# Queries and keys loaded with their tokens in columns, and split from SBUF, in a fused attention and two-block kernel

## The chip, the core and the metric

The kernel runs on one core of a Trainium2 chip, as one program. The metric is the device time of an execution in microseconds. Three timed runs of the kernel before gave 903.86, 904.44 and 904.83 us, so the median is 904.44.

Engine names in the profile: PE is TensorE (PEld its weight loads), DVE is VectorE, ACT is ScalarE, POOL is GpSimd, SP is the engine whose queue issues every DMA of this kernel.

## The reference

Four batches of eight heads, 576 tokens, 64 columns each; the inputs are float32 except the weights, which are float64. Attention has a causal mask and a decay made from a running sum of log f. Its output, 2304 tokens of 512 columns, goes through two feed-forward blocks.

```python
scores = q @ k.T / sqrt(64)
cum = cumsum(log(clip(f, 1e-4, 1)), -1)
scores = where(causal, -1e9, scores + cum[..., :, None] - cum[..., None, :])
attn = exp(scores - max(scores)); attn = attn / (sum(attn) + 1e-9)
x = (attn @ v).transpose(0, 2, 1, 3).reshape(2304, 512)
h = x @ w_in                                   # 512 -> 1024
solu = h * softmax(h); x = layernorm(solu) * g_ln @ w_out
h = maximum(x @ w2_in, 0); out = h * h @ w2_out  # 512 -> 2048 -> 512
```

Products have to be nearly exact in float32. The kernel gets that by splitting each float32 operand in two: hi, its leading bits, and lo, the rest. Three products, hi by lo, lo by hi and hi by hi, stand for one.

## The kernel before

**Tiles.** A query tile is 128 tokens of one batch, or the 64 that are left over at a seam of two batches: 20 tiles, 16 of 128 tokens and 4 of 64. For each tile the kernel goes through the eight heads. A head has scores (L478), the row's least value (L498), the exponentials with their sum (L512), the division by the sum on GpSimd (L539), transposes of the probabilities (L555) with a copy out of PSUM, and, for two heads at a time, the product with the values (L578). When 128 tokens of x are complete, the first block's work for them follows between the heads of later tiles: w_in (L762 to L764), softmax and norm, transposes (L839), w_out (L703 to L705). The second block (L1034 to L1066) runs after attention; its weights are converted at the seam of the two phases, in the places that keys and others leave.

**Queries and keys.** For scores, TensorE contracts over the 64 columns of a head, so queries and keys must lie with those columns in partitions. `load` (L348) brings a tile's keys, queries and values with tokens in partitions, into KN, QN (two buffers each) and VN. `transposed` (L363) turns four blocks of 128 columns, each holding a pair of heads, on TensorE into one PSUM slot of a ring of three. `prep_k` (L390) and `prep_q` (L426) then make from PSUM what the scores need:

- hi of the even heads and of the odd heads: K1[j] and Q1[i][j], in the pair's own half of the partitions, by a copy on ScalarE or VectorE (the query's one with the scale). The other half of K1 holds two rows of cum, which `auxrows` loads (L411).
- lo of each: K2[j] in the same half, Q2[i][j] in the opposite half, by a subtraction on VectorE (L419, L442).
- a duplicate of hi beside lo: in K2 in the opposite half, in Q2 in the same half, by `dup` (L380) on GpSimd or by a DMA from SBUF to SBUF.

One matmul then contracts hi with hi and the cum rows, and a second one the two cross products.

**The order.** Each instruction is a step of a plan (`Plan`, L28): it names its engine or engines, a duration, a priority, what it reads and what it writes. `lay` puts the steps in time by those durations and by fixed delays between engines, least priority value first among the steps that can start, and each engine and the DMA queue get their instructions in that order. The durations, delays and priorities are the program's own assumptions, and no engine leaves its order at run time: an instruction that waits holds up all behind it on its engine. Where a step can run on several engines, `lay` picks. Keys of the next tile are made from head PK (0) of the current tile on, queries from head PQ (6) on; loads go two tiles ahead.

Of the kernel before, what the change touches and what calls it, by code (L numbers as in the profile page):

```python
# [27 lines left out]
class Plan:  # L28
    """Puts the instructions in the order in which each engine is to take them.

    A step runs on one engine (or one of several), holds it for a time, and names what it reads and
    writes; from these come its dependencies, as if the steps ran in the order they were added. The
    steps are then laid out in time, the least `prio` first among those that can start, and emitted in
    the order of their starts. A step may take a PSUM slot of a ring, free again after its last user.
    """
# [21 lines left out]
    def add(self, eng, fn, prio, reads=(), writes=(), take=None, uses=(), late=0):  # L57
        """eng: {engine: ns}; take: the key of a slot that this step is the first to use; uses: keys of slots;
        late: what its consumers wait beyond the usual, if less then only on other engines."""
# [1204 lines left out]
```

## Time and profile before

| | |
|---|---|
| timed runs, us | 903.86, 904.44, 904.83 |
| profiled execution, span from first to last instruction, us | 902.2 |
| busy TensorE, VectorE, ScalarE, GpSimd, us | 856.1, 504.7, 478.0, 323.0 |
| mean granted TensorE clock | 0.994 |
| DMA queue q1: packets, MB | 97488, 64.88 |
| chain that ended last | PE 78%, DVE 11%, ACT 4%, POOL 3%, issue 3%, DMA 1% |

The profile gives the profiled execution's span and no other time for it; the median of the timed runs lies 2.2 us above it. A busy time counts the stretch from an instruction's start to its end, and TensorE's matmuls overlap, so a busy TensorE need not be one at its peak. In a row of the view by stretch, each engine has its busy us and in brackets the number of instructions. In a row of the timeline, equal instructions that follow each other are merged: start, length up to the last one's end, and the count. A wait row names the instruction that waited and the one that let it go.

### The profile page before, as it was taken

To read this page: it belongs to the slowest core of one execution; us is meant where nothing else is said; L and a number is where in the kernel's file an instruction comes from. 1 tells how busy PE (TensorE), PEld (TensorE's weight loads), DVE (VectorE), ACT (ScalarE), POOL (GpSimd) and SP (SyncE) were. 2 spreads that over 40 slices of the span, in tenths; PEclk is the share of its full clock that TensorE was granted. 3 is DMA by queue.
4 is the path that set the end of the run, shared out by engine and by line. 5 is a ranking of instruction groups with operands and counts; after the bars stand their busy time and mean duration, and the time that the engine had idled before them with its cause. 6 is when DMAs were issued, how large, how long until landed. Compare 5 with 4: busy or idle time off the path is not lost.

```text
span 902.2 us, 15952 instructions
## 1 busy us (share of the span) xinstructions
PE 856.1 (95%) x5440; PEld 734.4 (81%) x5440; DVE 504.7 (56%) x1463; ACT 478.0 (53%) x1242; POOL 323.0 (36%) x502
## 2 busy tenths in 40 slices
PE   4889999999999999999989787999999999999998
PEld 3567787888888888888879676899989999899997
DVE  8998777665776667765599889322222222222221
ACT  6788766667666666665667666223322322322322
POOL 7988743333333444432588778200000000000000
PEclk9999999999999999999999999999999999999999
DMA  8634331122311224010546643005102002000000
GB/s 220 171 99 114 95 84 41 43 65 56 76 42 43 59 62 97 26 48 25 164 144 191 202 139 117 1 1 167 43 1 71 36 1 71 36 1 0 36 1 36
DMA packets 97569, 65.90 MB, mean 73 GB/s; under 512 B 63408, under 2 KB 87472, under 8 KB 97488
## 3 DMA queue, kind: packets, MB, share of 16 engines
q1 hardware_dynamic: 97488, 64.88, 24.7%
q8 instruction: 43, 0.70, 0.3%
q14 instruction: 38, 0.31, 0.1%
HBM read 48.98 MB, written 14.30 MB: 70 GB/s over the span
## 4 chain that ended last, share of the span: by engine, by line
PE 78%; DVE 11%; ACT 4%; POOL 3%; issue 3%; DMA 1%; SPq 0%; POOLq 0%; ACTq 0%; DVEq 0%
PE pp L1034 6%; PE pp L1035 6%; PE pp L1036 6%; PE xo L578 6%; PE z L478 6%; PE pp L555 6%; PE pp L703 3%; PE hp L762 3%; PE hp L764 3%; PE hp L763 3%; PE pp L704 3%; PE pp L705 3%; PE z L1064 2%; PE z L1066 2%; PE hp L1064 2%
## 5 line engine op out<-in xcount | busy, mean ns | idle before, releaser
L1045 DVE CAST q<-q 128x384 fp32r<-128x384 f32 x96 | 40.5, 422 | 252.6 <-PE pp L1066 92.2
L1042 ACT ACTIVATE q<-pp 128x384 f32<-128x384 f32 x96 | 47.0, 490 | 232.4 <-PE pp L1036 230.5
L539 POOL TENSOR_SCALAR adj<-adj,st 128x128 f32<-128x128 f32 (+9 forms) x160 | 92.1, 578 | 176.1 <-DVE st L535 85.4
L512 ACT ACTIVATE adj<-z,st 64x288 f32<-64x288 f32 (+9 forms) x192 | 95.7, 501 | 34.3 <-DVE st L498 20.1
L478 PE MATMUL z<-k,q 128*128 128x256 f32 (+8 forms) x384 | 95.5, 342 | 6.6 <-ACT adj L512 6.4
L278 ACT COPY pt<-pp 128x256 f32<-128x256 f32 (+5 forms) x170 | 69.0, 423 | 48.2 <-PE pp L555 45.6
L703 PE MATMUL pp<-ln,woh 128*128 128x256 f32 x288 | 84.4, 293 | 0.4 <-POOL woh L282 0.4
L555 PE MATMUL pp<-ident,adj 128*128 128x128 f32 (+1 forms) x480 | 77.3, 274 | 6.2 <-POOL adj L539 3.2
L498 DVE CUSTOM_DVE_ANT_0 z<-z,maskb 128x128 f32<-128x128 f32 (+8 forms) x144 | 65.9, 460 | 28.0 <-PE z L478 26.4
L704 PE MATMUL pp<-ln,wol 128*128 128x256 f32 x288 | 81.1, 282 | 0.1
L705 PE MATMUL pp<-ln,woh 128*128 128x256 f32 x288 | 81.2, 282 | 0.0
L555 PEld LDWEIGHTS pp<-ident,adj 128*128 128x128 f32 (+1 forms) x480 | 53.1, 141 | 26.2 <-POOL adj L539 9.9
L578 PE MATMUL xo<-pt,vn 128*64 128x128 f32 (+3 forms) x960 | 73.6, 276 | 0.1
L578 PEld LDWEIGHTS xo<-pt,vn 128*64 128x64 f32 (+1 forms) x960 | 49.0, 136 | 26.1 <-issue 19.0
L478 PEld LDWEIGHTS z<-k,q 128*128 128x128 f32 (+1 forms) x384 | 56.8, 183 | 16.4 <-ACT adj L512 10.7
L762 PE MATMUL hp<-wih,xl 128*128 128x512 f32 x144 | 61.8, 429 | 0.5 <-ACT hp L801 0.5
L764 PE MATMUL hp<-wih,xh 128*128 128x512 f32 x144 | 57.3, 398 | 0.0
L763 PE MATMUL hp<-wil,xh 128*128 128x512 f32 x144 | 57.2, 397 | 0.0
L703 PEld LDWEIGHTS pp<-ln,woh 128*128 128x128 f32 x288 | 54.3, 188 | 2.8 <-issue 1.0
L704 PEld LDWEIGHTS pp<-ln,wol 128*128 128x128 f32 x288 | 54.3, 189 | 0.8 <-DVE wol L637 0.3
L705 PEld LDWEIGHTS pp<-ln,woh 128*128 128x128 f32 x288 | 54.2, 188 | 0.0
L1044 ACT ACTIVATE q<-q 128x384 f32<-128x384 f32 x96 | 50.4, 525 | 2.5
(481 smaller groups left out, 2263.7 us busy)
## 6 DMA issues: line engine op xcount, KB each, us to landing
x2d<-xc SPq DMA_DIRECT2D x72, 128.0 KB
pt<-in_moe_w_in_dram SPq DMA_DIRECT2D x22, 256.0 KB
pt<-in_moe_w_out_dram SPq DMA_DIRECT2D x22, 256.0 KB
ln<-x2d SPq DMA_DIRECT2D x24, 192.0 KB
out_dram<-pt SPq DMA_DIRECT2D x18, 256.0 KB
kn<-in_k_dram SPq DMA_DIRECT2D x16, 256.0 KB
qn<-in_q_dram SPq DMA_DIRECT2D x16, 256.0 KB
vn<-in_v_dram SPq DMA_DIRECT2D x16, 256.0 KB
```

The costliest lines, as they stand in the source:

```text
L278: nc.scalar.copy(dst(), src())
L478: nc.tensor.matmul(dst, lhsT=ql[:, p, 0:m], rhs=rhs, start=(g == 0), stop=(g == 1))
L512: nc.scalar.activation(out=adj[0:m, c[1] : c[2]], in_=Z[c[0]][0:m, 0 : c[2] - c[1]], func=AF.Exp, bias=st[0:m, low : low + 1], scale=-1.0, ...
L539: nc.gpsimd.tensor_scalar(out=adj[0:m, 0:ext], in0=adj[0:m, 0:ext], scalar1=st[0:m, 5:6], scalar2=1.0, op0=ALU.mult, op1=ALU.mult,)
L555: nc.tensor.transpose(at(sk)[:, (c - g) * m : (c - g + 1) * m], adj[0:m, zc : zc + P], ident[0:m, 0:m])
L578: nc.tensor.matmul(XO[own[j], p, off : off + m], lhsT=VN[vslot[b, c]][0:r, (2 * p + j) * D : (2 * p + j + 1) * D], rhs=pts[j][0:r, c * m : ...
L703: nc.tensor.matmul(px, lhsT=woh[:, fc, w], rhs=lo, start=(fc == 0), stop=False)
L704: nc.tensor.matmul(px, lhsT=wol[:, fc, w], rhs=hi, start=False, stop=False)
L705: nc.tensor.matmul(px, lhsT=woh[:, fc, w], rhs=hi, start=False, stop=(fc == KF - 1))
L762: nc.tensor.matmul(HP[:, c], lhsT=XL[i][:, cc, :], rhs=wih[:, cc, w], start=(cc == 0), stop=False)
L763: nc.tensor.matmul(HP[:, c], lhsT=XH[i][:, cc, :], rhs=wil[:, cc, w], start=False, stop=False)
L764: nc.tensor.matmul(HP[:, c], lhsT=XH[i][:, cc, :], rhs=wih[:, cc, w], start=False, stop=(cc == KC - 1))
```

## The change

The program's inputs q and k are handed over with tokens in the last dimension, as [batch, head, 64, 576]; that rearrangement of the inputs is no part of the device's time, and values are as before. `load` brings a tile's keys and queries in two DMAs each, one for the even heads into the lower 64 partitions and one for the odd heads into the upper 64, each row a run of 128 (or 64) tokens. `transposed` and `dup` are gone. `prep_k` and `prep_q` read KN and QN in SBUF instead of PSUM: copies may now go to GpSimd as well, lo is a subtraction of two SBUF operands, the duplicate of a query's hi is a second scaled copy from QN, and every duplicate of a key's hi is a DMA. The head at which queries of the next tile start goes from 6 to 4. Comments were taken out too; most lines of the program move by some 14.

```diff
-    KN = [new(f"kn{i}", [DM]) for i in range(2)]
-    QN = [new(f"qn{i}", [DM]) for i in range(2)]
+    KN = [new(f"kn{i}", [NP, P]) for i in range(2)]
+    QN = [new(f"qn{i}", [NP, P]) for i in range(2)]
...
         def dma(dst, src):
             def fn():
-                nc.sync.dma_start(
-                    dst[0:m].rearrange("p (h d) -> p h d", d=D), src[b, :, q0 : q0 + m, :].rearrange("h s d -> s h d")
-                )
+                for j in range(2):
+                    nc.sync.dma_start(
+                        dst[own[j], :, 0:m], src[b, :, :, q0 : q0 + m].rearrange("(p j) d s -> j d p s", j=2)[j]
+                    )
             return fn
...
-    def transposed(src, m, prio, reads):
...
-    def dup(m, dst, src, prio, reads, writes, by_dma):
...
     def prep_k(n, prio):
...
-        sk, tp = transposed(KN[n % 2], m, prio, [("kn", n % 2)])
+        raw = KN[n % 2]
         for j in range(2):
             rows = slice(0, P) if fresh else own[j]
             copy(
-                NP * m, lambda j=j, rows=rows: K1[j][rows, :, cs], lambda rows=rows: tp()[rows], prio + 1, [sk],
-                kcells("kh", j, kc, kc + m) + (kcells("ka", j, kc, kc + m) if fresh else []), [sk],
+                NP * m, lambda j=j, rows=rows: K1[j][rows, :, cs], lambda rows=rows: raw[rows, :, 0:m], prio + 1,
+                [("kn", n % 2)], kcells("kh", j, kc, kc + m) + (kcells("ka", j, kc, kc + m) if fresh else []),
+                psum=False,
             )
...
-                    out=K2[j][own[j], :, cs], in0=tp()[own[j]], in1=K1[j][own[j], :, cs].bitcast(F32), op=ALU.subtract
+                    out=K2[j][own[j], :, cs], in0=raw[own[j], :, 0:m], in1=K1[j][own[j], :, cs].bitcast(F32),
+                    op=ALU.subtract,
                 )
+            def dup(j=j):
+                nc.sync.dma_start(K2[j][other[j], :, cs].bitcast(F32), K1[j][own[j], :, cs].bitcast(F32))
...
+            pl.add(dict(dma=3.6 * m), dup, prio + 2, hk, kcells("kd", j, kc, kc + m))
...
     def prep_q(n, prio):
...
-        sk, tp = transposed(QN[i], m, prio, [("qn", i)])
         for j in range(2):
             copy(
-                NP * m, lambda j=j: q1[j][own[j], :, 0:m], lambda j=j: tp()[own[j]], prio + 1, [sk], [("qh", i, j)],
-                [sk], SC,
+                NP * m, lambda j=j: q1[j][own[j], :, 0:m], lambda j=j: raw[own[j], :, 0:m], prio + 1, [("qn", i)],
+                [("qh", i, j)], (), SC, False,
+            )
+            copy(
+                NP * m, lambda j=j: q2[j][own[j], :, 0:m], lambda j=j: raw[own[j], :, 0:m], prio + 2, [("qn", i)],
+                [("qd", i, j)], (), SC, False,
             )
...
-                    out=q2[j][other[j], :, 0:m], in0=tp()[own[j]], scalar=SC,
+                    out=q2[j][other[j], :, 0:m], in0=raw[own[j], :, 0:m], scalar=SC,
                     in1=q1[j][own[j], :, 0:m].bitcast(F32), op0=ALU.mult, op1=ALU.subtract,
...
-PK, PQ = 0, 6
+PK, PQ = 0, 4
...
+        if name in ("q", "k"):
+            a = a.transpose(0, 1, 3, 2)
```

The plan makes a new order from these steps. These places show it. Names end in the program's buffer numbers: in the keys' and queries' buffers k_8 and k_9 are K1 of even and odd heads, k_10 and k_11 their K2, q_12 to q_15 are Q1, q_16 to q_19 Q2, kn and qn the loaded tiles.

TensorE in the middle of attention, before: first-block matmuls (L703 to L705), a transposed query tile, and the scores of one head.

```order
L704 MATMUL pp_124<-ln_56_709,wol_74 128x256
L705 MATMUL pp_124<-ln_56_709,woh_73 128x256
L371 MATMUL pp_125<-ident_67,qn_22_89 128x128 x4
L478 MATMUL z_120<-k_8_75,q_14_81 128x288
L478 MATMUL z_120<-k_10_77,q_18_85 128x288
L703 MATMUL pp_124<-ln_56_710,woh_73 128x256
L704 MATMUL pp_124<-ln_56_709,wol_74 128x256
```

The same scores in the changed program, where L689 to L691 are the first-block matmuls and L464 the scores:

```order
L690 MATMUL pp_125<-ln_56_729,wol_74 128x256
L691 MATMUL pp_125<-ln_56_729,woh_73 128x256
L464 MATMUL z_119<-k_8_75,q_14_81 128x288
L464 MATMUL z_119<-k_10_77,q_18_85 128x288
L689 MATMUL pp_125<-ln_56_730,woh_73 128x256
L690 MATMUL pp_125<-ln_56_729,wol_74 128x256
```

The group of four transposes is gone, and the matmuls stand next to each other; the PSUM slot that it took is free for others.

The DMA queue at the start, before (L1105 stores the two parts of cum, L411 loads them into K1, L355 loads queries and keys, L605 words of w_in):

```order
L605 DMA ln_52_170<-in_moe_w_in_dram 128x1024
L355 DMA kn_21_88<-in_k_dram 128x8x64
L1105 DMA cumd<-pt_53_172 32x576
L1105 DMA cumd<-pt_53_177 32x576
L355 DMA qn_23_90<-in_q_dram 128x8x64
L411 DMA k_8_75<-cumd 2x4x128
L411 DMA k_9_76<-cumd 2x4x128
```

And now (L409 is a duplicate of keys, L1091 a store of cum, L357 the loads, L395 the cum rows of K1, L363 values):

```order
L591 DMA ln_52_165<-in_moe_w_in_dram 128x1024
L409 DMA k_10_77<-k_8_75 64x4x128
L1091 DMA cumd<-pt_52_163 32x576
L409 DMA k_11_78<-k_9_76 64x4x128
L357 DMA kn_21_88<-in_k_dram 64x4x128 x2
L1091 DMA cumd<-pt_53_170 32x576
L357 DMA qn_23_90<-in_q_dram 64x4x128 x2
L395 DMA k_8_75<-cumd 2x4x128
L395 DMA k_9_76<-cumd 2x4x128
```

The first tile's duplicates stand ahead of the two stores of cum, and each load of keys or queries is two DMAs.

VectorE at the start, before (L1128 is the running sum, L1134 the lo part of cum, L419 and L442 the subtractions for lo):

```order
L1125 MEMSET adj_30_97 32x576
L1128 SCALAR_TENSOR_TENSOR adj_32_99<-adj_30_97,adj_31_98 32x576
L419 TENSOR_TENSOR k_10_77<-pp_123,k_8_75 64x4x128
L1134 TENSOR_TENSOR pt_53_177<-adj_32_99,pt_53_172 32x576
L419 TENSOR_TENSOR k_11_78<-pp_123,k_9_76 64x4x128
L442 SCALAR_TENSOR_TENSOR q_16_83<-pp_124,q_12_79 64x512
L442 SCALAR_TENSOR_TENSOR q_17_84<-pp_124,q_13_80 64x512
```

And now (L1114, L1120, L403, L432 are the same; L285 is a copy of a key tile's hi):

```order
L1111 MEMSET adj_30_97 32x576
L285 CAST k_9_76<-kn_20_87 128x4x128
L1114 SCALAR_TENSOR_TENSOR adj_32_99<-adj_30_97,adj_31_98 32x576
L403 TENSOR_TENSOR k_10_77<-kn_20_87,k_8_75 64x4x128
L403 TENSOR_TENSOR k_11_78<-kn_20_87,k_9_76 64x4x128
L1120 TENSOR_TENSOR pt_53_170<-adj_32_99,pt_52_163 32x576
L432 SCALAR_TENSOR_TENSOR q_16_83<-qn_22_89,q_12_79 64x512
L432 SCALAR_TENSOR_TENSOR q_17_84<-qn_22_89,q_13_80 64x512
```

A copy of keys moved ahead of the running sum, and both subtractions of the first key tile ahead of the lo part of cum.

The queue in the middle of attention, before (L737 stores x2, L386 is a duplicate of queries):

```order
L737 DMA x2d<-xc_1220 128x256 x2
L355 DMA qn_22_89<-in_q_dram 128x8x64
L355 DMA kn_21_88<-in_k_dram 128x8x64
L737 DMA x2d<-xc_1220 128x256 x4
L355 DMA qn_23_90<-in_q_dram 128x8x64
L386 DMA q_19_86<-q_15_82 64x512
L737 DMA x2d<-xc_1220 128x256 x2
```

And now, at a like place (L723 stores x2, L363 loads values, L409 is a duplicate of keys):

```order
L723 DMA x2d<-xc_1115 128x256 x2
L363 DMA vn_27_94<-in_v_dram 128x8x64
L409 DMA k_10_77<-k_8_75 64x4x128
L409 DMA k_11_78<-k_9_76 64x4x128
L723 DMA x2d<-xc_1115 128x256
L357 DMA kn_20_87<-in_k_dram 64x4x128 x2
L357 DMA qn_23_90<-in_q_dram 64x4x128 x2
```

Stores of x2 stand between loads in both; now each tile's two duplicates of keys stand in the queue too, and are issued only after the stores ahead of them.

## Rows read from the trace of the kernel before

**Rows 1.** Stretches: us; busy PE, PEld, DVE, ACT, POOL (count); clock; DMA share; GB/s.
```profile
12.00:40.00 28.00, 20.10 (x92) 13.77 (x92) 26.07 (x79) 20.73 (x61) 25.18 (x31) 1.00 0.75 209
40.00:65.00 25.00, 22.70 (x148) 16.59 (x146) 23.55 (x76) 21.54 (x59) 21.84 (x32) 1.00 0.43 116
65.00:102.00 37.00, 33.81 (x269) 25.96 (x267) 31.23 (x95) 30.32 (x79) 30.70 (x49) 0.95 0.41 111
102.00:437.00 335.00, 334.43 (x2656) 279.39 (x2656) 226.56 (x831) 220.54 (x629) 129.52 (x223) 1.00 0.21 56
437.00:570.00 133.00, 112.97 (x627) 98.93 (x626) 115.29 (x214) 86.61 (x228) 107.47 (x145) 0.97 0.49 158
```

**Rows 2.** PE's waits from 102 to 437 us: total, times, longest us.
```profile
PE pp L703 <- POOL woh L282: 0.4, 1, 0.4
```

**Rows 3.** Line 371, 102 to 437 us: count, min/median/max ns, first/last start.
```profile
L371 PE MATMUL pp<-ident,kn x56: 222/272/328, 103.5 to 379.0; 128*128 128x128 f32 x48, 64*128 64x64 f32 x8
L371 PE MATMUL pp<-ident,qn x56: 222/272/329, 119.6 to 396.4; 128*128 128x128 f32 x48, 64*128 64x64 f32 x8
```

**Rows 4.** PE in order of time: start us, us to last end, operation, count.
```profile
204.87 0.42 PE L478 MATMUL z<-k,q 128*128 128x288 f32 x2
205.13 0.28 PE L703 MATMUL pp<-ln,woh 128*128 128x256 f32 x1
205.25 0.28 PE L704 MATMUL pp<-ln,wol 128*128 128x256 f32 x1
...
205.83 0.60 PE L371 MATMUL pp<-ident,qn 128*128 128x128 f32 x4
206.19 0.51 PE L478 MATMUL z<-k,q 128*128 128x288 f32 x2
206.54 0.28 PE L703 MATMUL pp<-ln,woh 128*128 128x256 f32 x1
...
276.93 0.46 PE L371 MATMUL pp<-ident,kn 64*128 64x64 f32 x4
277.32 0.73 PE L478 MATMUL z<-k,q 128*128 128x512 f32 x2
```

**Rows 5.** The chain of waits from 12 to 40 us, shares by line.
```profile
by line: DVE ln L627 14.4%; DVE wil L637 13.7%; DVE z L498 10.6%; POOL ln L633 9.3%; issue 7.5%; DVE k L419 6.9%; DVE ln L623 6.6%; DVE q L442 5.0%; POOL ln L282 4.9%; POOL adj L539 4.1%; DVE st L535 2.9%; DVE st L498 2.7%; DVE st L529 2.4%
```

**Rows 6.** VectorE from 12 to 102 us; last two rows: busy us, mean ns.
```profile
L419 DVE TENSOR_TENSOR k<-pp,k x10: 409/680/695, 12.0 to 79.9; 64x512 fp32r<-64x512 f32 x6, 64x256 fp32r<-64x256 f32 x4
L442 DVE SCALAR_TENSOR_TENSOR q<-pp,q x10: 418/684/692, 15.9 to 85.8; 64x512 fp32r<-64x512 f32 x6, 64x256 fp32r<-64x256 f32 x4
...
L627 DVE SCALAR_TENSOR_TENSOR ln<-ln 128x512 uint32<-128x512 uint32 x7 | 6.7, 958 | 0.1
L637 DVE TENSOR_TENSOR wil<-ln,wih 128x512 fp32r<-128x512 f32 x6 | 5.6, 940 | 1.6 <-ACT wih L278 1.6
```

**Rows 7.** Copies on ScalarE and GpSimd over the whole span, by line.
```profile
L278 ACT CAST k<-pp x37: 358/581/606, 5.6 to 380.6; 64x512 fp32r<-64x512 f32 x20, 128x512 fp32r<-128x512 f32 x10, 128x256 fp32r<-128x256 f32 x4, 64x256 fp32r<-64x256 f32 x3
L278 ACT CAST wih<-ln x8: 611/618/622, 13.1 to 47.4; 128x512 fp32r<-128x512 f32 x8
...
L388 POOL TENSOR_SCALAR k<-k x35: 401/616/1074, 6.4 to 381.2; 64x512 fp32r<-64x512 f32 x31, 64x256 fp32r<-64x256 f32 x4
```

**Rows 8.** The start, in order of time.
```profile
4.53 1.08 PE L371 MATMUL pp<-ident,kn 128*128 128x128 f32 x4 [4.53 <-DMA kn<-in_k_dram]
...
7.36 0.96 DVE L1134 TENSOR_TENSOR pt<-adj,pt 32x576 fp32r<-32x576 f32 x1
...
10.16 0.29 SPq L411 DMA_DIRECT2D k<-cumd  x1
...
12.51 0.78 PE L478 MATMUL z<-k,q 128*128 128x256 f32 x2
```

**Rows 9.** The DMA queue's own waits.
```profile
SPq L737 <- DVE xc L284: 83.9, 8, 17.6
```

**Rows 10.** PE's waits from 437 to 570 us.
```profile
PE hp L1064 <- DVE qn L1048: 9.1, 8, 1.6
```

More of the change, by code (lines that the diff above doesn't have):

```diff
@@ L196, in tile_kernel @@
     nc = tc.nc
-    B, H, S, D = q.shape
+    B, H, D, S = q.shape
     NT, DM = out.shape
@@ L362, in load @@
         pl.add(ns, dma(QN[n % 2], q), prio + 1, writes=[("qn", n % 2)])
-        pl.add(ns, dma(VN[n % NV], v), max(prio + 2, V0), writes=[("vn", n % NV)])
-    def transposed(src, m, prio, reads):
-        sk = key()
-        def fn():
-            tp = at(sk).rearrange("p (c x) -> p c x", x=P)
-            for p in range(NP):
-                nc.tensor.transpose(tp[:, p, 0:m], src[0:m, p * P : p * P + P], ident[0:m, 0:m])
-        pl.add(dict(pe=NP * 109 * m / P), fn, prio, reads=reads + ["ident"], writes=[sk], take=sk)
-        return sk, lambda: at(sk).rearrange("p (c x) -> p c x", x=P)[:, :, 0:m]
+        pl.add(ns, vals, max(prio + 2, V0), writes=[("vn", n % NV)])
     def fill(dst, x, prio, writes):
@@ L380, in fill @@
         s = pl.add(dict(pool=460, dve=600), fn, prio, [], writes)
-    def dup(m, dst, src, prio, reads, writes, by_dma):
-        def fn():
-            if s.on == "dma":
-                nc.sync.dma_start(dst().bitcast(F32), src())
-            else:
-                nc.gpsimd.tensor_scalar(out=dst(), in0=src(), scalar1=1.0, scalar2=1.0, op0=ALU.mult, op1=ALU.mult)
-        ns = dict(pool=161 + 0.833 * NP * m, dma=max(350, 3.0 * m))
-        if by_dma:
-            ns.pop("pool")
-        s = pl.add(ns, fn, prio, reads, writes)
     def prep_k(n, prio):
@@ L419, in lo @@
                 nc.vector.tensor_tensor(
-                    out=K2[j][own[j], :, cs], in0=tp()[own[j]], in1=K1[j][own[j], :, cs].bitcast(F32), op=ALU.subtract
-                )
+                    out=K2[j][own[j], :, cs], in0=raw[own[j], :, 0:m], in1=K1[j][own[j], :, cs].bitcast(F32),
+                    op=ALU.subtract,
+                )
+            def dup(j=j):
+                nc.sync.dma_start(K2[j][other[j], :, cs].bitcast(F32), K1[j][own[j], :, cs].bitcast(F32))
             hk = kcells("kh", j, kc, kc + m)
-            pl.add(dict(dve=67 + 1.045 * NP * m), lo, prio + 2, [sk] + hk, kcells("kl", j, kc, kc + m), uses=[sk])
-            dup(
-                m, lambda j=j: K2[j][other[j], :, cs], lambda j=j: K1[j][own[j], :, cs].bitcast(F32), prio + 2, hk,
-                kcells("kd", j, kc, kc + m), DUPK0 <= n < DUPK1,
+            pl.add(
+                dict(dve=67 + 1.045 * NP * m), lo, prio + 2, [("kn", n % 2)] + hk, kcells("kl", j, kc, kc + m)
             )
+            pl.add(dict(dma=3.6 * m), dup, prio + 2, hk, kcells("kd", j, kc, kc + m))
     def prep_q(n, prio):
@@ L442, in lo @@
                 nc.vector.scalar_tensor_tensor(
-                    out=q2[j][other[j], :, 0:m], in0=tp()[own[j]], scalar=SC,
+                    out=q2[j][other[j], :, 0:m], in0=raw[own[j], :, 0:m], scalar=SC,
                     in1=q1[j][own[j], :, 0:m].bitcast(F32), op0=ALU.mult, op1=ALU.subtract,
                 )
-            pl.add(dict(dve=67 + 1.045 * NP * m), lo, prio + 2, [sk, ("qh", i, j)], [("ql", i, j)], uses=[sk])
-            dup(
-                m, lambda j=j: q2[j][own[j], :, 0:m], lambda j=j: q1[j][own[j], :, 0:m].bitcast(F32), prio + 2,
-                [("qh", i, j)], [("qd", i, j)], DUPQ0 <= n < DUPK1,
-            )
+            pl.add(dict(dve=67 + 1.045 * NP * m), lo, prio + 2, [("qn", i), ("qh", i, j)], [("ql", i, j)])
     def head(s):
@@ L1223 @@
 AHEAD = 10000.0
-DUPK0, DUPQ0, DUPK1 = 20, 20, 4
 V0, LOAD1 = -15000.0, 3000.0
@@ L1250 @@
     for name in _INS:
-        a = _np.ascontiguousarray(inputs[name])
+        a = inputs[name]
+        if name in ("q", "k"):
+            a = a.transpose(0, 1, 3, 2)
+        a = _np.ascontiguousarray(a)
         if a.dtype == _np.float64:
```

6 lines of the change are left out of this document (5 added, 1 removed).

## The prediction

> **What bounds the kernel now.** I read busy time by stretch first, then TensorE's own waits, then single instructions. The reader should see three kinds of stretch [rows 1]. From 12 to 102 us TensorE is not full (20.10 of 28, 22.70 of 25, 33.81 of 37 us), while VectorE has 26.07 of 28 us from 12 to 40. From 102 to 437 us TensorE has 334.43 of 335 us at a granted clock of 1.00, and its only wait there is one of 0.4 us [rows 2]; VectorE has 68%, ScalarE 66%, GpSimd 39%. From 437 to 570 us it has 112.97 of 133 us: the second block's weights are converted there, VectorE has 115.29 us, and TensorE's largest wait is 9.1 us for VectorE [rows 10]. Behind that nothing of this change runs. So work taken from TensorE pays in the middle stretch alone, and work put on VectorE, GpSimd or the queue costs in the first.
>
> A busy TensorE row overlaps its neighbours: matmuls of 0.28 us start 0.12 us apart [rows 4]. What an instruction costs is the distance to the next start, not its length.
>
> **The change part by part.**
>
> *Transposes out of TensorE.* Each of 20 query tiles has a group of four for its keys and one for its queries, 40 groups. 28 of them lie from 103.5 to 396.4 us: 96 transposes of 128 tokens and 16 of 64, so 24 full groups and 4 half ones [rows 3]. A full group starts at 205.83 and the next instruction at 206.19: 0.36 us. The pair of score matmuls behind it takes 0.35 us to the next start (206.19 to 206.54), the same pair behind an ordinary matmul 0.26 (204.87 to 205.13), so the group costs another 0.09 after it has gone. A half group takes 0.39 (276.93 to 277.32) [rows 4]. The sum is 24 x 0.45 + 4 x 0.39 = 12.4 us. Where another transpose stands beside the group the 0.09 stays, so the low end is 24 x 0.36 + 4 x 0.39 = 10.2. I take 12.4, since most groups stand beside scores or first-block matmuls. The 12 groups before 102 us I count at nothing: TensorE waits there for others. At the high end the eight of them that come after the first two tiles (four full, four half) count too: 4 x 0.45 + 4 x 0.39 = 3.4.
>
> *Copies out of PSUM become copies out of SBUF.* On ScalarE a cast of 512 columns out of SBUF has a median of 0.618 us, one out of PSUM 0.581 over its forms [rows 7]: +0.04 us each, and in the order of the changed program ScalarE has 50 of them where it had 72. GpSimd loses its 64 duplicates and gets 61 copies of the same size, VectorE goes from 8 copies to 9, and 40 duplicates go by DMA where 16 did. In the middle stretch a third of VectorE's and ScalarE's time is free and hides all this: 0. In the first stretch the engines' sums are about level: 0, bounds -1 and +1.
>
> *The subtractions for lo.* There are 80 on VectorE, as before, but both inputs now lie in SBUF; before, one lay in PSUM. With one in PSUM the 20 that lie in 12 to 102 us have medians of 0.680 and 0.684 and never take more than 0.695. The two kinds of 512 columns with both inputs in SBUF have means of 0.958 and 0.940 us in the same stretch [rows 6]. I read this as VectorE being held by GpSimd, which is busy 77.72 of those 90 us [rows 1]. The extra is up to 0.958 - 0.684 = 0.27 us each. VectorE's lines have about two thirds of the chain from 12 to 40 us [rows 5] and, with ScalarE and TensorE busier, less later. I take eight of the 20 at the full extra, +2 us; the bounds are 0 (none is held, or others hide it) and 20 x 0.27 = +5.4. In the middle 56 of them add 15 us to VectorE, which then has 242 of some 323 us, 75%: hidden. [...]
>
> *The start.* In the queue the first duplicate now stands ahead of the first store of cum and the second between the two stores; on VectorE a cast stands ahead of the scan, and both subtractions for lo ahead of the lo part of cum, where one stood. That part started at 7.36 us and the first scores at 12.51 [rows 8]. Both go back by one subtraction (0.68), less what the keys are earlier without their transposes: their group took 1.08 us to its last end [rows 8]. As the conversions of w_in fill part of the time, I take +0.5; bounds -0.5 and +1.
>
> *Duplicates of keys by DMA.* They add a landing between the copy of hi and the first scores of the next tile. From the issue of the cum rows at 10.16 us to the scores that waited for them at 12.51 are 2.35 us, two issues and a landing [rows 8]; GpSimd did a duplicate in 0.62 [rows 7]. So hi reaches its second place some 1.7 us later. The copies are planned from the tile's first head on, and a tile lasts 335 us / 14 = 24 us in the middle, so this is covered, except where a new batch waits for the old one's key columns (three places). I take +0.5; bounds 0 and +3.
>
> *The loads* have runs of 512 bytes in place of 256, so fewer packets; the DMA engines are at 0.21 in the middle [rows 1]: nothing. *The end*, 437 to 570 us, starts when attention ends and moves with it; the placement of its conversions on engines changes a little: 0, bounds -2 and +2.
>
> Sum: -12.4 + 2 + 0.5 + 0.5 = -9.4 us. On the profiled span of 902.2 that is 892.8. The timed runs lie 2.2 us above that span in the median (904.44), so 895.0 in the runs.
>
> **Rivals.**
> 1. *Duplicates late in the queue: slower.* The queue is served in order, and behind the stores of x2 it now holds duplicates that the next tile's first scores need. One kind of store waited 83.9 us in 8 times, 17.6 at most [rows 9]. If a duplicate is issued only when such a store is free, the first scores of a tile stall TensorE with everything behind them. It decides from 12.4 / 14 = 0.9 us per tile start on. With four of the 14 starts losing 4 us, 16 us less the 12.4 gives 904.4 + 3.6 = 908. For it: TensorE takes instructions strictly in order. Against it: loads of keys already passed the same queue and TensorE waited for none of them in the middle. 10%.
> 2. *VectorE held at full strength in the first stretch.* All 20 subtractions lose 0.27 and the start 1 us: -12.4 + 5.4 + 1 + 0.5 gives 899. For it: VectorE at 26.07 of 28 us. Against it: from 65 to 102 us TensorE has 91% and VectorE 84%, so VectorE no longer leads. 15%.
> 3. *The middle isn't bound by TensorE's throughput.* Waits shorter than the overlap (0.28 less 0.12 us) show nowhere; if they fill the place that the transposes leave, little is gained: 903 to 905. Against it: the starts stand evenly 0.12 apart. 7%.
> 4. *The first stretch gains too.* Fewer users of the three PSUM slots and an emptier TensorE: -12.4 - 3.4 with none of the costs gives 888.6. 8%.
>
> **How the numbers follow.** The forecast has 60%, with its own range of 890 to 899. The range for all runs from 888 (gains of 12.4, 3.4 and 0.5) to 904 (a gain of 10.2 against costs of 5.4, 1 and 3, with 0.4 over), and leaves out rival 1 and part of rival 3. A difference under 0.2% (1.8 us) can't be told from none. Faster: forecast, rivals 2 and 4, 83%. Same: rival 3, 7%. Slower: rival 1, 10%.
>
> **What would show it.** The stretch in which TensorE has no wait is about 12 us shorter, with the same matmuls at the same distances. The subtractions for lo spread from 0.68 up to over 1 us before 100 us, and stay at no cost behind it. TensorE becomes full at 102 to 106 us; later than that means rival 2. I am wrong if TensorE's waits between 100 and 430 us sum to more than about 3 us: for a DMA or the queue at a tile's first scores that is rival 1; and if the steady stretch is as long as before without such waits, rival 3.

## The result, and the profile after

The changed kernel takes 913.01 us in the median of four runs (912.15 to 913.44), the kernel before, timed beside it, 904.25 (903.86 to 904.83): 1.0094 times as long, 95% interval 1.0080 to 1.0109. Slower, where 895.0 was forecast and 904 was the end of the range.

Stretches of the kernel after, with the columns of [rows 1]; the last four lie within the fourth (a DMA share counts packets by their start, so it can pass 1):

```profile
12.00:40.00 28.00, 14.09 (x47) 8.71 (x48) 25.42 (x62) 16.94 (x47) 21.11 (x22) 1.00 0.93 230
40.00:65.00 25.00, 19.70 (x115) 13.06 (x114) 23.90 (x71) 18.69 (x53) 22.74 (x29) 1.00 0.36 91
65.00:102.00 37.00, 29.03 (x195) 20.21 (x196) 32.03 (x94) 29.63 (x77) 31.93 (x50) 1.00 0.34 95
102.00:437.00 335.00, 329.88 (x2592) 273.12 (x2593) 232.30 (x836) 213.93 (x622) 148.90 (x233) 0.98 0.25 65
138.00:143.00 5.00, 3.86 (x30) 2.87 (x29) 4.77 (x20) 3.96 (x17) 3.99 (x8) 1.00 1.16 250
140.00:145.00 5.00, 3.69 (x23) 2.43 (x22) 4.23 (x23) 4.32 (x16) 4.14 (x6) 0.80 0.75 172
145.00:150.00 5.00, 5.00 (x23) 3.70 (x22) 2.88 (x14) 2.64 (x11) 1.45 (x3) 0.50 0.71 185
150.00:155.00 5.00, 5.00 (x31) 4.18 (x29) 3.21 (x14) 3.12 (x10) 1.86 (x4) 0.67 0.59 136
```

Against [rows 1], TensorE is emptier in all three stretches before 102 us (62.8 us busy where it had 76.6; the 12 groups of transposes that lay there make some 5 of it, 8 x 0.45 + 4 x 0.39), while VectorE is as full as it was (81.4 and 80.9), with fewer instructions done (227 where it had 250). From 102 to 437 us TensorE is no longer full.

TensorE's waits, before 102 us (first three rows) and from 102 to 437 us: total, times, longest:

```profile
PE pp L541 <- POOL adj L525: 14.8, 16, 3.6
PE z L464 <- DMA k<-cumd: 14.5, 1, 14.5
PE z L464 <- ACT adj L498: 8.6, 8, 3.7
...
PE pp L541 <- POOL adj L525: 2.7, 6, 0.7
PE z L464 <- ACT adj L498: 1.5, 3, 0.6
```

The second is the wait for the first scores, at 14.51 us where they were at 12.51 [rows 8]; ahead of them on VectorE, start and us, stand the running sum, the first two subtractions and the lo part of cum:

```profile
5.41 1.75 DVE L1114 TENSOR_TENSOR_SCAN adj<-adj,adj 32x576 f32<-32x576 f32 x1
7.09 2.04 DVE L403 TENSOR_TENSOR k<-kn,k 64x512 fp32r<-64x512 f32 x2
9.17 0.74 DVE L1120 TENSOR_TENSOR pt<-adj,pt 32x576 fp32r<-32x576 f32 x1
```

The first of the waits is new in its size: the norms on GpSimd (L525), for which TensorE's transposes wait. In the kernel before, up to 102 us:

```profile
PE z L478 <- ACT adj L512: 6.4, 6, 2.5
PE pp L555 <- POOL adj L539: 3.2, 8, 1.0
```

The subtractions for lo and that of the weights, VectorE from 0 to 102 us: busy us, mean ns:

```profile
L403 DVE TENSOR_TENSOR k<-kn,k 64x512 fp32r<-64x512 f32 x8 | 9.9, 1237 | 1.0 <-POOL k L283 0.5 <-ACT k L279 0.4
...
L623 DVE TENSOR_TENSOR wil<-ln,wih 128x512 fp32r<-128x512 f32 x6 | 7.2, 1202 | 0.0
...
L432 DVE SCALAR_TENSOR_TENSOR q<-qn,q 64x512 fp32r<-64x512 f32 x8 | 6.2, 780 | 0.3
L403 DVE TENSOR_TENSOR k<-kn,k 64x256 fp32r<-64x256 f32 x4 | 3.8, 947 | 0.1
```

In [rows 6] the keys' and queries' 512-column forms stand near 0.68 us. Not only they grew: w_in's subtraction (L623), whose inputs were in SBUF before too, went from 0.940 to 1.202.

**Where the time went.** Each query tile forms its xl with one VectorE instruction (L591 before, L577 after), so its start is a mark of progress. Lags below are its start minus that of the kernel before (34.8, 51.3, 94.8, 193.6 and 441.1 us at tiles 0, 1, 3, 8 and 19), one profiled execution each.

| us | tile 0 | 1 | 3 | 8 | 19 |
|---|---|---|---|---|---|
| after | 4.1 | 9.4 | 14.9 | 14.9 | 8.8 |

So 14.9 us are lost by 95 us and 6.1 of them won back by 441; behind that nothing happens. In the other account, each 1 us stretch is split into TensorE idle time, busy time lost to a granted clock under 1.00 (busy times one minus the clock), and the rest, work at full clock:

| us | idle to 102 | clock | idle 102-437 | clock | idle behind | clock | work in all |
|---|---|---|---|---|---|---|---|
| before | 21.9 | 1.7 | 0.6 | 0.0 | 23.7 | 3.3 | 851.1 |
| after | 39.2 | 0.0 | 5.1 | 5.0 | 25.0 | 1.7 | 834.3 |

TensorE does lose some 17 us of work (16.8 in this account). It idles 23.1 us more, and the clock takes 1.7 more. The idle time is read directly; the clock's part is an upper estimate, since matmuls overlap. e9 and e17 below have TensorE's instructions in the same order and come to 837.1 and 841.4 us of work, so the split between clock and work is good to some 4 us.

The clock's loss in the middle lies at one place: GpSimd, VectorE and TensorE of the kernel after, start and us:

```profile
138.03 1.73 POOL L283 TENSOR_SCALAR k<-kn 64x512 fp32r<-64x512 f32 x2
```

```profile
138.60 1.70 DVE L403 TENSOR_TENSOR k<-kn,k 64x512 fp32r<-64x512 f32 x2
```

```profile
141.92 0.27 PE L541 MATMUL pp<-ident,adj 64*128 64x64 f32 x1 [0.73 <-POOL adj L525]
142.60 0.45 PE L464 MATMUL z<-k,q 128*64 128x256 f32 x2 [0.41 <-ACT adj L498]
```

At the seam of two batches (tiles of 64 tokens, little work a head) GpSimd copies keys from SBUF while VectorE subtracts them from SBUF. Both take some 0.86 us an instruction, and the norms stand behind. Up to 143 us the granted clock is 1.00, and TensorE is busy 3.86 of the last 5 us, with a wait of 0.73 us for a norm and one of 0.41 for exponentials. Then the clock is 0.50 up to 150 us, and 0.67 in the mean from 150 to 155. What brings it down isn't shown. It falls without GpSimd's copies too: the clock takes 1.7 us from 102 to 437 us in e8, and 4.4 and 4.8 in e10 and e11, near the same seam.

### The profile page after: what moved, and what is told of

Read it like the earlier page. It is cut to its first block, busy times and chain, and to the rows that moved or that the text cites. A ratio compares the mean times of both kernels' runs of the same rounds, so it can differ in the third digit from the quotient of the medians.

```text
span 910.3 us, 15617 instructions
## 1 busy us (share of the span) xinstructions
PE 841.0 (92%) x5280; PEld 716.8 (79%) x5280; DVE 517.0 (57%) x1458; ACT 468.9 (52%) x1225; POOL 344.1 (38%) x500
## 4 chain that ended last, share of the span: by engine, by line
PE 71%; DVE 13%; POOL 7%; issue 5%; ACT 2%; DMA 1%; SPq 0%; POOLq 0%; ACTq 0%; DVEq 0%
PE pp L1020 6%; PE pp L1022 6%; PE pp L1021 6%; PE pp L541 6%; PE xo L564 6%; PE z L464 5%; PE hp L748 3%; PE pp L689 3%; PE hp L750 3%; PE hp L749 3%; PE pp L691 3%; PE pp L690 3%; PE hp L1050 2%; PE hp L1051 2%; PE hp L1052 2%
## 5 line engine op out<-in xcount | busy, mean ns | idle before, releaser
L525 POOL TENSOR_SCALAR adj<-adj,st 128x128 f32<-128x128 f32 (+9 forms) x160 | 99.5, 625 | 143.7 <-DVE st L521 80.1
L464 PE MATMUL z<-k,q 128*128 128x256 f32 (+8 forms) x384 | 93.1, 343 | 24.7 <-DMA k<-cumd 14.5
L279 ACT COPY pt<-pp 128x256 f32<-128x256 f32 (+5 forms) x177 | 72.7, 427 | 54.9 <-PE pp L541 52.6
L541 PE MATMUL pp<-ident,adj 128*128 128x128 f32 (+1 forms) x480 | 80.0, 279 | 18.0 <-POOL adj L525 17.5
L464 PEld LDWEIGHTS z<-k,q 128*128 128x128 f32 (+1 forms) x384 | 58.6, 188 | 35.2 <-ACT adj L498 15.4
L689 PE MATMUL pp<-ln,woh 128*128 128x256 f32 x288 | 83.9, 291 | 0.5 <-DVE ln L828 0.5
L691 PE MATMUL pp<-ln,woh 128*128 128x256 f32 x288 | 81.4, 283 | 0.0
L689 PEld LDWEIGHTS pp<-ln,woh 128*128 128x128 f32 x288 | 54.8, 190 | 2.6 <-DVE ln L828 0.9
L691 PEld LDWEIGHTS pp<-ln,woh 128*128 128x128 f32 x288 | 54.7, 190 | 0.0
```

The costliest lines, as they stand in the source:

```text
L279: nc.scalar.copy(dst(), src())
L464: nc.tensor.matmul(dst, lhsT=ql[:, p, 0:m], rhs=rhs, start=(g == 0), stop=(g == 1))
L525: nc.gpsimd.tensor_scalar(out=adj[0:m, 0:ext], in0=adj[0:m, 0:ext], scalar1=st[0:m, 5:6], scalar2=1.0, op0=ALU.mult, op1=ALU.mult,)
L541: nc.tensor.transpose(at(sk)[:, (c - g) * m : (c - g + 1) * m], adj[0:m, zc : zc + P], ident[0:m, 0:m])
L689: nc.tensor.matmul(px, lhsT=woh[:, fc, w], rhs=lo, start=(fc == 0), stop=False)
L691: nc.tensor.matmul(px, lhsT=woh[:, fc, w], rhs=hi, start=False, stop=(fc == KF - 1))
```

## The experiments

Theory A: VectorE's subtractions with both inputs in SBUF and GpSimd hold each other up, in a stretch that these two bound. Rivals: B, the key duplicates by DMA hold up the queue and the loads of w_in; C, the plan's new order. In the edits, tiles in KOLD, QOLD and KPOOL have keys and queries loaded, transposed and duplicated as before the change; empty sets are the changed kernel.

| run | us | against before, 95% | tile 0 | 1 | 3 | 8 | 19 |
|---|---|---|---|---|---|---|---|
| e2 first six tiles old | 904.17 | 0.9997-1.0017 | 0.1 | 0.7 | 6.4 | 6.7 | 1.4 |
| e3 old, duplicates by DMA | 912.41 | 1.0083-1.0132 | 1.5 | 0.8 | 11.1 | 9.0 | 8.8 |
| e4 duplicates on GpSimd too | 917.36 | 1.0134-1.0164 | 2.1 | 8.7 | 13.3 | 16.3 | 13.9 |
| e5 first ten old, PQ 6 | 900.51 | 0.9949-0.9974 | 0.1 | 0.8 | 1.1 | 2.8 | -2.7 |
| e6 first six old, PQ 6 | 899.34 | 0.9938-0.9968 | 0.2 | 0.7 | 1.3 | 0.2 | -4.5 |
| e7 changed, PQ 6 | 912.75 | 1.0085-1.0115 | 4.1 | 9.3 | 14.9 | 15.2 | 8.9 |
| e8 no copies on GpSimd | 908.95 | 1.0041-1.0071 | 3.5 | 8.3 | 10.8 | 9.5 | 5.3 |
| e9 e6 and e8 together | 898.04 | 0.9923-0.9962 | 0.2 | 0.3 | 0.5 | -1.9 | -6.2 |
| e10 e8, first six lifted to PSUM | 904.41 | 0.9998-1.0018 | 1.5 | 6.9 | 9.2 | 5.8 | 1.9 |
| e11 e8, first six duplicates off DMA | 909.75 | 1.0050-1.0082 | 2.0 | 6.5 | 10.1 | 9.7 | 6.2 |
| e12 e10 and e11 together | 905.27 | 1.0003-1.0022 | 2.4 | 0.2 | 4.1 | 4.9 | 0.6 |
| e13 e9, first six queries changed | 905.71 | 1.0010-1.0031 | -1.3 | 6.5 | 9.8 | 5.7 | 1.7 |
| e14 e9, first six keys changed | 907.17 | 1.0025-1.0059 | 2.2 | 4.0 | 8.9 | 6.5 | 2.5 |
| e15 e9, dearer subtraction in the plan | 897.81 | 0.9924-0.9963 | 0.4 | 0.3 | 0.3 | 0.1 | -7.0 |
| e16 e9's order, subtractions from SBUF | 905.88 | 1.0001-1.0033 | 2.3 | 5.3 | 7.0 | 7.2 | 2.8 |
| e17 e9's order, duplicates by DMA | 903.70 | 0.9987-1.0006 | 4.8 | 5.1 | 5.9 | 3.9 | -0.1 |
| e18 e16 and e17 together | 908.05 | 1.0031-1.0071 | 5.4 | 6.1 | 7.9 | 8.4 | 4.1 |

**e1, the instructions by themselves.**

```diff
+nc.vector.tensor_tensor(out=lo, in0=raw, in1=hi, op=subtract)   # or in0 in PSUM
+nc.gpsimd.tensor_scalar(out=adj, in0=adj, scalar1=one, ...)     # beside it, or not
```

> This kernel computes nothing of the reference: it runs the VectorE subtraction of 64 partitions x 512 columns 16 times in each of several stretches: with both inputs in SBUF, with one in PSUM, and as a plain copy, each alone and then beside GpSimd norms (128x512) or GpSimd copies (64x512), and once beside key-like duplicates by DMA. Theory A (the subtraction with two SBUF inputs and GpSimd hold each other up): 0.68 to 0.70 us alone in both forms; beside GpSimd the two-SBUF form goes to 1.0 us or more on average and GpSimd's own instruction grows from 0.6-0.7 to over 1 us too, while the form with one PSUM input stays at 0.68-0.72. Theory B (the DMA traffic, not GpSimd, stretches it): about 0.70 beside GpSimd, clearly more beside the DMA duplicates.

One execution was taken. The stretches ran into each other, but some are pure. VectorE, start and us of so many instructions; from 61 to 71 us beside GpSimd, from 76 to 87 beside GpSimd with one input in PSUM, from 117 to 127 beside DMAs at a busy share of 0.99 with GpSimd idle:

```profile
61.04 10.31 DVE L63 TENSOR_TENSOR lo<-raw,hi 64x512 fp32r<-64x512 f32 x10
...
76.22 10.76 DVE L66 TENSOR_TENSOR lo<-praw,hi 64x512 fp32r<-64x512 f32 x15
...
116.69 10.74 DVE L63 TENSOR_TENSOR lo<-raw,hi 64x512 fp32r<-64x512 f32 x15
```

And GpSimd in the first and the second of them:

```profile
62.29 1.00 POOL L75 TENSOR_SCALAR adj<-adj,one 128x512 f32<-128x512 f32 x1
63.26 1.04 POOL L78 TENSOR_SCALAR gout<-raw 64x512 fp32r<-64x512 f32 x1
...
78.07 0.68 POOL L75 TENSOR_SCALAR adj<-adj,one 128x512 f32<-128x512 f32 x1
78.84 0.62 POOL L78 TENSOR_SCALAR gout<-raw 64x512 fp32r<-64x512 f32 x1
```

A subtraction from SBUF takes 0.72 us from start to start beside DMAs with GpSimd idle, 1.03 beside GpSimd, and GpSimd's norm goes from 0.68 to 1.00 or 1.19, its copy from 0.62 to 1.04 or 0.94, by turns. With one input in PSUM neither loses anything (0.72, 0.68 and 0.62). So what theory A supposes is measured here, and it costs both sides; beside DMAs the subtraction takes no more than with an input in PSUM. By an estimate from these rows, one instruction after the other would make 0.68 for the subtraction and 0.65, the mean of GpSimd's two, 1.33 us a pair; 1.03 were measured, so the two run side by side in part.

**e2, e6, e5: the old preparation where VectorE and GpSimd have no slack.**

```diff
+KOLD = QOLD = KPOOL = range(6)     # e2, e6; range(10) in e5
+PK, PQ = 0, 6                      # e5, e6; 4 in e2, as in the changed kernel
```

> The changed kernel, but the keys and queries of the first six query tiles (those prepared before 102 us) come with tokens in rows and go through TensorE and PSUM as before the change, their copies on GpSimd; the other fourteen tiles stay changed. Theory A (VectorE and GpSimd hold each other up in the first stretch, which they bound): TensorE's idle time before 102 us falls from 39 us to 22-26 us, the subtractions before 102 us go back to means near 0.6 us for the keys, and the time is 893 to 899 us, faster than both kernels. Theory C (the loss lies in the middle: norms late, a clock dip, the plan's order): the first stretch recovers little and the time is 905 to 913.

> As the run before with the first six tiles old, but with PQ at 6 in place of 4, so that the order up to some 60 us is that of the kernel before. If the 6.4 us that that run had lost by tile 3 came from the order that PQ 4 gives (theory C), the lag at tile 3 is now under 2 us and the time 897 to 901 us; if it came from the changed tiles (theory A), tile 3 still lags 4 us or more and the time is 902 to 906 us.

> Keys and queries of query tiles 0 to 9 as before the change (rows, TensorE, PSUM, copies by GpSimd), of tiles 10 to 19 changed, and the priority number PQ of queries back at 6: up to tile 9 every engine has the order of the kernel before. Theory A (the change costs only where VectorE and GpSimd have no slack, up to about 225 us, and gains behind): the lag of the step that forms a query tile's xl is 0 up to tile 9 and falls to -7 to -9 us by tile 19, the time is 895 to 898 us. Theory C (the loss came from the plan's order and could appear anywhere): 900 to 906 us.

e2 missed A's time by 5 us: idle time before 102 us came back (22.3 us), but 6.4 us were lost by tile 3 with the operations of before. e6 shows whose they were: with PQ 6 as before, 1.3 at tile 3 and 899.34 us. So the order that PQ gives is worth some 5 us where the preparation is old (C, in part), and it works by the clock: up to 102 us TensorE idles 22.3 us in both runs, but the clock takes 7.8 us in e2 and 3.1 in e6. In the changed kernel e7 finds nothing in PQ. e6 and e5 beat both kernels: changed tiles pay where they come after 100 us. e5 came out slower than A's forecast, in C's range, and its gain from tile 8 to 19 is 5.5 us where 7 to 9 were expected.

**e3, e4, e7, e8: one part alone.**

```diff
+KOLD = QOLD = range(20); PQ = 6    # e3: before the change, all key duplicates by DMA
+KPOOL = range(20)                  # e4: changed, key duplicates on GpSimd or by DMA
+PK, PQ = 0, 6                      # e7: changed
+COPYPOOL = False                   # e8: changed, copies from SBUF on ScalarE or VectorE only
```

> The kernel before with one part of the change alone: the keys' copies to the other partitions go by DMA in all twenty tiles; the transposes, the PSUM inputs and the copies of the queries stay as before. Theory A: GpSimd loses some 0.4-0.6 us a copy in the first stretch, so 901 to 905 us, no slower than before. Theory B (the duplicates by DMA fill the queue and are late): 907 to 912 us, most of the loss of the changed kernel.

> The changed kernel, but the keys' copies to the other partitions may go on GpSimd or by DMA as the plan finds earlier, as they did before the change. Theory A: no gain, GpSimd gets work back in a stretch that it bounds: 912 to 920 us. Theory B: most of the loss comes back: 899 to 906 us.

> The changed kernel with PQ at 6 as before, and nothing else. Theory C (the order that PQ 4 gives is a part of the loss): 903 to 909 us. Theory A alone: 911 to 916 us, no gain.

> The changed kernel, but the copies from the loaded keys and queries (hi, and the queries' second copy) go on ScalarE or VectorE only, never on GpSimd: some 40 instructions of 0.7 us leave GpSimd in the middle and 9 to 11 before 102 us. Theory A: GpSimd's norms come earlier, TensorE's waits for them fall from 14.8 to under 10 us before 102 us and from 2.7 to under 1 us behind, 903 to 909 us. If GpSimd isn't what holds it (VectorE or the DMAs do): 912 to 918 us, since VectorE or ScalarE take the work.

e3 went against A and for B: duplicates by DMA alone cost 8.5 us, all of it by tile 3. Up to 102 us TensorE idles 4.9 us more than in the kernel before, and the clock takes 6.9 us where it took 1.7; the plan's order is new in e3 too, so the 8.5 us aren't the queue's alone. e4 shows that taking them back to GpSimd is dearer still, as A says. e8 gave 4.1 us by tile 3: GpSimd's copies of 512 columns, 0.85 us and more each, stood ahead of its norms. TensorE's waits for norms fell from 14.8 to 10.5 us before 102 us, from 2.7 to 1.1 from 102 to 437 us, a little less than A had (under 10 and under 1):

```profile
PE pp L600 <- POOL adj L584: 10.5, 12, 2.4
```

```profile
PE pp L600 <- POOL adj L584: 1.1, 1, 1.1
```

**e10, e11, e12: take both suspects from the changed kernel (with e8's edit).**

```diff
+LIFT = range(6)   # e10, e12: ScalarE copies raw to a PSUM slot; hi, copies and lo read it there
+KACT = range(6)   # e11, e12: key duplicates from raw by ScalarE or VectorE
```

> The changed kernel with no copies on GpSimd (908.95 us) and one more edit: for the first six query tiles ScalarE first lifts the loaded keys and queries into a PSUM slot (0.6 us each, twelve of them), from which hi, the copies and the subtractions read, so that the subtractions have one input in PSUM as before the change; loads in columns and key duplicates by DMA stay. Theory A (VectorE's subtractions with two SBUF inputs and GpSimd hold each other up): the subtractions before 102 us go back to 0.69 us, the lag at tile 3 falls from 10.8 to 4-7 us, 902 to 906 us. Theory B (the key duplicates by DMA make the loads of the first weights late): 908 to 914 us, no gain.

> The changed kernel with no copies on GpSimd (908.95 us) and one more edit: the key duplicates of the first six query tiles are made by ScalarE or VectorE from the loaded keys instead of by DMA (twelve instructions of 0.35 to 0.6 us); the subtractions keep two SBUF inputs. Theory B: the DMAs' busy share from 12 to 40 us falls from 0.93 to about 0.75, the last load of the first weights is issued 3 us sooner, lag at tile 3 down from 10.8 to 5-7 us, 903 to 906 us. Theory A: 908 to 914 us, since VectorE gets no relief.

> Both edits of the two runs before: first six tiles lifted into PSUM and their key duplicates by ScalarE or VectorE. If both causes are real and add up: 898 to 903 us, lag at tile 3 of 0 to 3 us. If ScalarE, which gets some 15 us more work before 102 us, becomes the bound: 905 us or more.

In e10 the subtractions before 102 us are back at their old length (line, busy us, mean ns):

```profile
L502 DVE SCALAR_TENSOR_TENSOR q<-pp,q 64x512 fp32r<-64x512 f32 x8 | 5.5, 689 | 1.3 <-ACT q L281 1.1
L452 DVE TENSOR_TENSOR k<-pp,k 64x512 fp32r<-64x512 f32 x8 | 5.5, 686 | 0.8 <-ACT k L279 0.7
```

The time falls by 4.5 us, as A had it, but tile 3 by 1.6 only, less than A had. e11 gives nothing in time and misses B's range, though it issues the last load of w_in 3.6 us sooner than e8; the DMAs' share from 12 to 40 us falls only to 0.88. Both edits together (e12) give 6.7 at tile 3 and 8.1 at tile 1, so each hides the other there. e12's time is no better than e10's and lies in the range named for ScalarE as the bound: ScalarE is busy 25.00 of the 28 us from 12 to 40 (17.89 in e8), and the clock takes 8.0 us in e12's middle, where e10 loses 4.4. Which of the two takes the gain isn't shown.

**e13, e14, e15: add one side to the best kernel, and let the plan know the price.**

```diff
+KOLD = KPOOL = range(6); QOLD = ()    # e13
+QOLD = range(6); KOLD = KPOOL = ()    # e14
+LOX = 350                             # e15: ns more for a subtraction from SBUF
```

> The kernel that gained most (first six tiles as before, the rest changed, no copies on GpSimd, 898.0 us), but with the queries of the first six tiles changed too: their subtractions get two inputs in SBUF, their second copy comes from SBUF on ScalarE or VectorE, and no DMA is added. Theory A (VectorE and GpSimd hold each other up): the lag at tile 3 is 3 us or more and the time 901 to 906 us. Theory B (only the key duplicates by DMA cost): lag under 2 us, 896 to 899 us.

> The same kernel with the keys of the first six tiles changed and their queries as before: subtractions with two SBUF inputs and key duplicates by DMA, both on the keys' side. Theory A alone: about what the queries alone cost, 901 to 906 us. Both causes: more than the queries alone, 904 to 909 us, with the last load of the first weights issued 3 us or more later than in the kernel before.

> The kernel that gained most, with the plan's cost of a subtraction with two SBUF inputs raised by 350 ns, to what the traces show beside GpSimd. If the 4.7 us that TensorE still idles from 102 to 437 us come from steps that the plan sets too early behind these subtractions: under 2 us of idle time there and 894 to 897 us. If they come from elsewhere: 897 to 901 us.

The queries alone, with no DMA added, cost 7.7 us against e9 and the keys 9.1; the two are not additive, since e8, with both, lies 10.9 above e9. In e14 the last load of w_in is issued at 35.55 us, in the kernel before at 31.08. e15 leaves 3.8 of the 4.7 us of idle time: the plan's price isn't why the middle gives less.

**e9, and e16 to e18: the best kernel, then its operations changed and the order kept.** e9 does not add up as hoped: without GpSimd's copies it gains 1.3 us on e6 and not 4, which can't be told from none, and its 898.04 us lie at the border of the two ranges named. TensorE's waits for norms in the middle stay at 1.3 us. e15 is no faster than e9 by what can be told. e16 to e18 settle what e2 had left open, for every engine's rows stand as in e9, but for the edit; e16 and e18 leave out the lo parts of the first six tiles.

```diff
-in0=tp()[own[j]]                             # e16, e18: PSUM
+in0=K1[j][own[j], :, cs].bitcast(F32)        # hi from SBUF; queries likewise; tiles 0 to 5
-nc.gpsimd.tensor_scalar(out=dst(), in0=src(), ...)
+nc.sync.dma_start(dst().bitcast(F32), src()) # e17, e18: the seven key duplicates on GpSimd
```

> The two edits that gained, together: the first six query tiles as before the change (with PQ 6), the other fourteen changed, and the copies from the loaded keys and queries never on GpSimd. If GpSimd's copies are what held the norms in the middle, its gain of 4 us adds to that of the first edit: 895 to 898 us, TensorE's waits for norms from 102 to 437 us under 1 us. If the plan's order gives and takes as much at random: 898 to 902 us.

> The kernel that gained most (898.0 us) with every engine's order kept: only the subtractions of the first six tiles read both inputs from SBUF (hi twice, so that the lo parts of these tiles are left out and come as zeros), in place of one from PSUM. Theory A (VectorE and GpSimd hold each other up, whatever the order): the subtractions before 102 us take 0.9 us or more on average, the lag at tile 3 is 3 us or more and the time 901 to 906 us. Theory C (any other order than the one before loses 6 to 10 us in the first stretch, and the operations themselves little): lag under 2 us, 897 to 900 us.

> The kernel that gained most, with the order kept: only the seven key duplicates of the first six tiles that GpSimd makes are issued as DMAs at the same place. Theory B (the duplicates by DMA make the loads of the first weights late): lag at tile 3 of 5 us or more, 902 to 907 us. Theory C: lag under 2 us, 896 to 900 us, or a little faster for the relief of GpSimd.

> Both edits of the two runs before, the order kept: subtractions with two SBUF inputs (lo parts of the first six tiles left out) and all key duplicates by DMA. Theories A and B: lag at tile 3 of 6 us or more, 904 to 910 us. Theory C: lag under 3 us, 897 to 901 us.

The subtractions in e9 (L502, L452) and e16 (L503, L452) before 102 us:

```profile
L502 DVE SCALAR_TENSOR_TENSOR q<-pp,q 64x512 fp32r<-64x512 f32 x8 | 5.5, 689 | 0.3
L452 DVE TENSOR_TENSOR k<-pp,k 64x512 fp32r<-64x512 f32 x8 | 5.5, 688 | 0.8 <-PE pp L385 0.3 <-ACT k L279 0.3
```

```profile
L503 DVE SCALAR_TENSOR_TENSOR q<-q 64x512 fp32r<-64x512 f32 x8 | 7.7, 963 | 0.2
L452 DVE TENSOR_TENSOR k<-k 64x512 fp32r<-64x512 f32 x8 | 7.3, 913 | 0.1
```

GpSimd's own duplicates of keys grew with them, e9 and e16:

```profile
L404 POOL TENSOR_SCALAR k<-k 64x512 fp32r<-64x512 f32 x7 | 5.1, 732 | 1.6 <-ACT k L279 1.1
```

```profile
L404 POOL TENSOR_SCALAR k<-k 64x512 fp32r<-64x512 f32 x7 | 5.9, 842 | 1.7 <-ACT k L279 1.2
```

TensorE's waits before 102 us in e9, then in e16:

```profile
PE z L538 <- ACT adj L572: 6.3, 6, 2.3
PE pp L615 <- POOL adj L599: 2.6, 6, 1.0
```

```profile
PE z L540 <- ACT adj L574: 8.6, 6, 4.1
PE pp L617 <- POOL adj L601: 4.5, 9, 1.3
```

By this edit alone tile 3 comes 6.5 us later and the time is 7.8 us longer. Up to 102 us TensorE idles 4.1 us more, and the clock takes 6.2 us where it took 3.2. In e17 the loads of w_in are issued late; e9, then e17:

```profile
3.21 0.97 SPq L665 DMA_DIRECT2D ln<-in_moe_w_in_dram  x1
11.40 2.25 SPq L665 DMA_DIRECT2D ln<-in_moe_w_in_dram  x4
```

```profile
7.31 0.59 SPq L665 DMA_DIRECT2D ln<-in_moe_w_in_dram  x1
17.35 2.04 SPq L665 DMA_DIRECT2D ln<-in_moe_w_in_dram  x4
```

The queue's own wait in e17, up to 42 us:

```profile
SPq L402 <- ACT k L279: 4.4, 2, 3.7
```

A duplicate at the head of the queue waits for its hi on ScalarE, and the load of the weights stands behind it: tile 0 lags 4.8 us, and the time is 5.7 us longer than e9's. That place is GpSimd's, not the one which the changed kernel's plan gives, where the four loads are issued at 13.89 us and 11.22 in the kernel before; e3 has the plan's own place (13.01). So A and B each cost 6 to 8 us in e9 with the order kept, and a new order (C) isn't needed for that. Together (e18) they cost 10.0 of the 15.0 us by which the changed kernel lies above e9; the rest is not taken apart.

## Why the prediction was wrong

The step that failed is the price of what the change puts into the first stretch: 3 us in the sum (2 + 0.5 + 0.5) and 9.4 at the range's end, where 14.9 us were lost by tile 3. The gain was counted about right, and half of it did not come through.

- *Bounds of the kernel.* Right: the work taken from TensorE is there (some 17 us over the whole span), and what is added costs in the first stretch. Wrong was what the costs come to, and how much of the gain is left in the time.
- *The subtractions for lo, +2 us (0 to +5.4).* This step priced VectorE's half, eight of 20 at 0.27 us. e16 measures 6.5 us at tile 3 and 7.8 in the end: the 512-column subtractions' means rise by 0.23 to 0.27 us, so most of them are hit (the full extra in e1 is 0.31), and GpSimd, which was counted at nothing, loses as much on its side (0.32 to 0.51 us an instruction in e1). TensorE waits 1.9 us more for norms and 2.3 for exponentials, and up to 3.0 us before 102 us are the clock's, for which the sum had no term. Rival 2, the same at full strength, still priced one engine alone.
- *Copies, 0 in the first stretch (-1 to +1).* GpSimd's copies from SBUF cost 4.1 us by tile 3 (e8, in a new order): 61 for 64 in number, 12 for 13 before 102 us, but they stand at other times, ahead of norms.
- *Duplicates by DMA, +0.5 (0 to +3).* 8.5 us alone (e3), 5.7 with the order kept (e17). The step looked for scores that wait for a duplicate, as rival 1 did, and TensorE has no such wait. What is late is behind the duplicates in the queue: the loads of w_in, in a stretch where the DMAs are near full (0.93 from 12 to 40 us). That these loads carry the whole cost isn't shown, since e11 issues the last of them sooner and gains nothing.
- *The loads, nothing.* The step looked at the DMAs' share in the middle alone. In the first stretch a load of keys is two DMAs, which take 1.37 us to issue where one took 0.41, the first load of w_in is issued at 4.56 us and not at 3.03, and without duplicates by DMA the DMAs' share from 12 to 40 us is still 0.88 (e11; 0.75 before). No run has the new loads alone, so their price stays open.
- *The start, +0.5.* The first scores come 2.0 us later, beyond the bound of +1. The step counted with 0.68 us a subtraction; beside GpSimd's copies the first two took 2.04 together and the running sum 1.75 where it took 1.34, so the lo part of cum starts at 9.17 us, not 7.36. Tile 0 lags 4.1; e13, which keeps the old keys, has -1.3 there; the rest wasn't taken apart.
- *Transposes out of TensorE, -12.4.* The work went about as counted, but 6.1 us of time came back between tiles 3 and 19, 6.7 in e9. The kernel before had almost no idle time there (0.6 us), so a late norm shows there, and a dip of the clock too. The test named beforehand, waits over 3 us from 100 to 430 us, was met (5.1 us idle). Of the waits, 3.3 us are for GpSimd (its norms 2.7) and 1.5 for exponentials; no rival had GpSimd as the cause.
- *The sum.* Costs in a stretch where VectorE, GpSimd and the DMAs are all near full were added as if each were small. They are neither small nor additive; the lag at tile 3 falls from 14.9 us to 10.8 without GpSimd's copies, to 9.2 with subtractions from PSUM as well, and to 4.1 without duplicates by DMA as well (e8, e10, e12).

What is left open: why e9's middle idles 4.7 us (GpSimd has 1.3 of it, ScalarE's exponentials 1.6), what the loads in columns cost, and the last 3.6 us at tile 3, 7.2 in the time, in e12 over e9.

## What to carry to other kernels

Moving an operand from PSUM to SBUF was not free for VectorE here, although the subtraction of 64 partitions by 512 columns takes 0.72 us from start to start in either form where nothing holds it up (e1): with both inputs in SBUF, it and GpSimd paid some 0.3 us or more each time they met (1.03 in place of 0.72). A change that frees one engine should be put in only where the engines that take its work have slack: the same edit is worth -4.3 us with the first six tiles left out and queries started at head 6 as before (e6), and +8.8 with all tiles in. With the first six left out and queries started at head 4 it is worth nothing (e2), as TensorE loses some 5 us more to the clock before 102 us. And what a DMA added to the queue made late here was what stood behind it: with seven duplicates by DMA (e17) four loads of w_in are issued at 17.35 us and not at 11.40, and the time is 5.7 us longer, while TensorE waits for no duplicate in the changed kernel.

## What the runs showed of the hardware

Plain casts on VectorE meet GpSimd too: of four of 128x512 from SBUF to SBUF beside it (e1), three took 0.42 or 0.43 us and one 0.84, while the norm on GpSimd beside the last three took 1.16 in place of 0.68. So beside this one norm, two casts paid nothing and one paid double. In the kernel after, TensorE's granted clock fell from 1.00 to 0.50 at 143 us, after 5 us of which it was busy 3.86, and was 0.50 in the mean from 143 to 148 us and from 148 to 153. By the account above e9 loses up to 11.5 us to the clock in all, 6.8 of them behind 437 us, and the kernel before 5.0, 3.3 of them there.
